# Issuing the weight loads of a decode layer in halves, from two DMA queues at the same time

## The chip, the cores and the metric

One core of one Trainium2 chip. The metric is the device time of the whole program on that core, in microseconds (us), lower is better. Some readings come from the trace's single records: the DMA packets (start, duration, bytes, queue) and the moments at which each of the 16 DMA engines reports its share of a load as landed. The trace doesn't number the engines, but on each engine a packet starts where the packet before it ended (to within about 20 ns), so one engine can be followed from packet to packet. These readings are given in plain tables; the profile's own lines stand in fences of their own.

## The reference, cut to what matters

One decode step for four sequences, in bfloat16: attention with a window of 2,048 cached keys, then a gated feed-forward layer. Nothing is used twice, so nearly all of the work is to read weights and cache once.

```python
def reference(A_x, A_k_cache, A_v_cache, A_wq, A_wo, B_x, B_w1, B_w3, B_w2):
    # x: 4 x 1 x 1024; k_cache, v_cache: 4 x 4 x 8192 x 128, the last 2048 keys count
    # wq: 1024 x 4096, wo: 4096 x 1024, w1, w3: 1024 x 3584, w2: 3584 x 1024
    h  = x + attention(layernorm(x), k_cache, v_cache, wq) @ wo
    n  = layernorm(h)
    return h + (silu(n @ w1) * (n @ w3)) @ w2
```

The core reads 55.6 MB for it: wq 8.4, K 8.4, V 8.4, wo 8.4, w1 7.3, w3 7.3, w2 7.3 MB.

## The kernel before

All big loads go through one ring buffer of 160 KiB per partition, in the order of a plan, all from the sync queue. A region is loaded again as soon as the matmuls that read it are done. Weights lie row after row inside a partition, so a load of m rows is one contiguous run per partition: 64 KiB for wo, 56 KiB for w1.

```python
    def load_rows(at, src, n, r0, m):
        t = ring[:, at : at + m * n]
        nc.sync.dma_start(out=t, in_=src[:, r0 * n : (r0 + m) * n])
        return [t[:, k * n : (k + 1) * n] for k in range(m)]
    # ... load_kv, load_side, load_tail: cut
    plan = [
        # ... wq in two loads, three small ones: cut
        ("k", load_kv, (64 * KIB, A_k_cache, 0)),
        ("k", load_kv, (96 * KIB, A_k_cache, 2)),
        ("v", load_kv, (128 * KIB, A_v_cache, 0)),
        ("v", load_kv, (0, A_v_cache, 2)),
        ("wo", load_rows, (32 * KIB, wo_v, D, 0, 32)),
        ("w1", load_rows, (96 * KIB, w1_v, N_F, 0, 8)),
        ("w3", load_rows, (0, w3_v, N_F, 0, 4)),
        ("w3", load_rows, (28 * KIB, w3_v, N_F, 4, 4)),
        ("w2", load_rows, (56 * KIB, w2_v, D, 0, 17)),
        ("w2", load_rows, (90 * KIB, w2_v, D, 17, 7)),
        ("w2", load_rows, (104 * KIB, w2_v, D, 24, 3)),
        ("w2", load_rows, (110 * KIB, w2_v, D, 27, 1)),
    ]
```

The end of the kernel (cut; comments added here):

```python
    gate_up("w1", g_ps)                               # 64 matmuls
    nc.scalar.activation(out=eg[:], in_=g_ps[:, :, :HF], func=ACT.Exp, scale=-1.0)
    nc.vector.tensor_scalar_add(out=eg[:], in0=eg[:], scalar1=1.0)
    nc.vector.reciprocal(out=eg[:], in_=eg[:])
    nc.vector.tensor_tensor(out=gs[:], in0=g_ps[:, :, :HF], in1=eg[:], op=ALU.mult)
    gate_up("w3", u_ps)                               # 64 matmuls
    nc.vector.tensor_tensor(out=hg[:], in0=u_ps[:, :, :HF], in1=gs[:], op=ALU.mult)
    nc.vector.transpose(out=hgT, in_=hg)              # then 112 matmuls with w2 into y2_ps
    nc.scalar.copy(out=res[:], in_=y2_ps[:])
    nc.scalar.dma_start(out=out_flat, in_=res)
```

Of the kernel before, what the change touches and what calls it, by code (L numbers as in the profile page):

```python
# [19 lines left out]
def kernel(  # L20
# [13 lines left out]
    nc = tc.nc  # L34

    B, _, D = A_x.shape
# [47 lines left out]
    wo_v = A_wo.rearrange("(p i) n -> p (i n)", i=IO)  # L84
    w1_v = B_w1.rearrange("(p i) n -> p (i n)", i=KC)
    w3_v = B_w3.rearrange("(p i) n -> p (i n)", i=KC)
    w2_v = B_w2.rearrange("(p i) n -> p (i n)", i=IF)
    ring = stream.tile([P, RING], BF16)

    def load_rows(at, src, n, r0, m):  # L90
# [2 lines left out]
        nc.sync.dma_start(out=t, in_=src[:, r0 * n : (r0 + m) * n])  # L93
        return [t[:, k * n : (k + 1) * n] for k in range(m)]

    def load_kv(at, src, b):

        out = []
        for k in range(BS):
            v = ring[:, at + k * JK * Dh : at + (k + 1) * JK * Dh]  # L100
            nc.sync.dma_start(
                out=v,
                in_=src[b + k, :, Sk - W : Sk, :].rearrange("g (pp j) d -> pp g (j d)", pp=PK),
            )
            out.append(v.rearrange("p (j d) -> p j d", d=Dh))
        return out

    N_Q, N_F = Hq * Dh, F
# [13 lines left out]
    def load_tail(at, src, n, r0, m):  # L122
# [4 lines left out]
    KIB = 512  # L127
# [4 lines left out]
        ("side", load_side, SETS[2]),  # L132
        ("wq", load_tail, (32 * KIB, wq_v, N_Q, 4, 4)),
        ("k", load_kv, (64 * KIB, A_k_cache, 0)),
        ("k", load_kv, (96 * KIB, A_k_cache, 2)),
        ("v", load_kv, (128 * KIB, A_v_cache, 0)),
        ("v", load_kv, (0, A_v_cache, 2)),
        ("wo", load_rows, (32 * KIB, wo_v, D, 0, 32)),
        ("w1", load_rows, (96 * KIB, w1_v, N_F, 0, 8)),
        ("w3", load_rows, (0, w3_v, N_F, 0, 4)),  # L140
        ("w3", load_rows, (28 * KIB, w3_v, N_F, 4, 4)),
        ("w2", load_rows, (56 * KIB, w2_v, D, 0, 17)),
        ("w2", load_rows, (90 * KIB, w2_v, D, 17, 7)),
        ("w2", load_rows, (104 * KIB, w2_v, D, 24, 3)),
        ("w2", load_rows, (110 * KIB, w2_v, D, 27, 1)),
    ]
# [3 lines left out]
    def load_next(n=1):  # L150
        for _ in range(n):
            if cursor[0] < len(plan):
                kind, f, args = plan[cursor[0]]
                loaded.setdefault(kind, []).extend(f(*args))
                cursor[0] += 1
# [19 lines left out]
    for c in range(2):  # L175
# [8 lines left out]
        out=xn[:], in0=x_sb[:], scalar1=mv[:, 0:1], scalar2=rstd[:, 0:1],  # L184
# [14 lines left out]
    for r0, ne, ns in SETS:  # L199
# [3 lines left out]
            out=xs[:, len(sl) : len(sl) + ns, : ne * 4].rearrange("b l (i s) -> b l i s", s=4),  # L203
            in_=v[:, KC - 1, :, :, :],
        )
        for l in range(ns):
            nc.tensor.transpose(
                out=ts_ps[: ne * 4, len(sl), :], in_=xs[:, len(sl), : ne * 4], identity=ident[:B, :B]
# [4 lines left out]
    for _, ne, ns in SETS:  # L213
# [14 lines left out]
        out=perm[:].rearrange("p (h dq) -> p h dq", dq=JG),  # L228
        in_=ident[:].rearrange("p (dq h) -> p h dq", dq=JG),
# [12 lines left out]
    for j in range(2, JG):  # L242
        nc.vector.tensor_tensor(
            out=same[:, 0, :], in0=same[:, 0, :], in1=ident[:, j * QD : (j + 1) * QD], op=ALU.add
# [6 lines left out]
    for kc in range(KC):  # L251
        wq_t = loaded["wq"][kc]
        for hf in range(CQ // 512):
            for g in range(JG):
                c0 = g * CQ + hf * 512
                n = min(512, N_Q - CE - c0) if kc == KC - 1 else 512
# [23 lines left out]
    for r in range(REP):  # L280
        nc.tensor.transpose(out=qt_ps[:, r, :], in_=q_sb[:, r * Dh : (r + 1) * Dh], identity=ident[:])
    nc.vector.tensor_copy(
        out=qz[:, :, : Hkv * QD].rearrange("p b (g z) -> p b g z", g=Hkv)[:, :, :, :REP],
        in_=qt_ps[:].rearrange("p r (g x) -> p x g r", g=Hkv)[:, :B, :, :],
# [10 lines left out]
    def emit_scores(u):  # L295
        b, n = units[u]
        kT_v = kT_tiles[u][:].rearrange("d j (pp g) -> d g j pp", g=Hkv)
        for g in range(Hkv):
            z0 = (b * Hkv + g) * QD
            nc.tensor.matmul(  # L300
                scores_ps[QD * g : QD * (g + 1), n * 512 : (n + 1) * 512],
                lhsT=qz_v[:, z0 : z0 + QD],
                rhs=kT_v[:, g, :, :],
                start=(b == 0),
                stop=(b == B - 1),
            )

    nt = 0
    for u, (b, n) in enumerate(units):
        k_v = loaded["k"][b]  # L310
        kT = ktpool.tile([P, NJ, P], BF16, tag="kT")
        for t in range(NJ // TB):
            kt_ps = psA.tile([P, TB, P], BF16, tag=f"kt{nt % 4}")
            for jj in range(TB):
                nc.tensor.transpose(  # L315
                    out=kt_ps[:, jj, :], in_=k_v[:, n * NJ + t * TB + jj, :], identity=ident[:]
                )
            if nt % 2 == 0:
                nc.vector.tensor_copy(out=kT[:, t * TB : (t + 1) * TB, :], in_=kt_ps[:])  # L319
            else:  # L320
                nc.scalar.copy(out=kT[:, t * TB : (t + 1) * TB, :], in_=kt_ps[:])  # L321
            nt += 1
        kT_tiles.append(kT)
        if u >= 1:
            emit_scores(u - 1)
        if u == NSB * BS - 1:
            load_next()
    emit_scores(len(units) - 1)


# [7 lines left out]
        out=Pm[:], in_=scores_ps[:], func=ACT.Exp, bias=nmax[:], scale=1.0, accum_out=rsum[:]  # L338
# [6 lines left out]
    for c in range(NSB):  # L345
# [4 lines left out]
        for g in range(Hkv):  # L350
            if g % 2 == 0:
                nc.vector.tensor_scalar(  # L352
                    out=z[:, :, g, :], in0=pt_ps[:], scalar1=mask[:, g : g + 1], scalar2=None, op0=ALU.mult
# [10 lines left out]
        out=Dm[:], in0=ident[:].rearrange("p (g b r) -> p b g r", g=Hkv, b=B),  # L364
# [38 lines left out]
    for i in range(IO):  # L403
# [34 lines left out]
        out=hn[:], in0=h1[:], scalar1=tot[:, 0:1], scalar2=rstd2[:, 0:1],  # L438
# [5 lines left out]
        out=hnT[:].rearrange("p k x -> p (k x)"), in_=hn[:].rearrange("q (c k) -> q k c", k=KC)  # L444
# [5 lines left out]
    def gate_up(kind, out_ps):  # L450
        for k in range(KC):
            for hf in range(2):
                for j in range(JG):
                    c0 = j * CF + hf * HF
                    nc.tensor.matmul(  # L455
                        out_ps[QD * j : QD * (j + 1), hf, :HF],
                        lhsT=hnT[:, k, :],
                        rhs=loaded[kind][k][:, c0 : c0 + HF],
                        start=(k == 0),
                        stop=(k == KC - 1),  # L460
                    )
            if kind == "w1" and k == RQ - 1:
                load_next(3)

    gate_up("w1", g_ps)
    eg = wide.tile([P, 2, HF], FP32, tag="w4k")
    nc.scalar.activation(out=eg[:], in_=g_ps[:, :, :HF], func=ACT.Exp, scale=-1.0)
    nc.vector.tensor_scalar_add(out=eg[:], in0=eg[:], scalar1=1.0)
    nc.vector.reciprocal(out=eg[:], in_=eg[:])  # L469
    gs = wide.tile([P, 2, HF], FP32, tag="w4k")  # L470
    nc.vector.tensor_tensor(out=gs[:], in0=g_ps[:, :, :HF], in1=eg[:], op=ALU.mult)
    gate_up("w3", u_ps)
    hg = act.tile([P, 2, HF], BF16)
    nc.vector.tensor_tensor(out=hg[:], in0=u_ps[:, :, :HF], in1=gs[:], op=ALU.mult)
# [3 lines left out]
        out=hgT[:].rearrange("p i x -> p (i x)"),  # L478
        in_=hg[:].rearrange("q s c -> q (s c)").rearrange("q (c i) -> q i c", i=IF),
# [47 lines left out]
```

## Time and profile before

| | before |
|---|---|
| time, median | 137.94 us (137.84 to 138.09, 4 runs) |
| span of the profiled run | 136.1 us |
| bytes moved, DMA packets | 55.75 MB, 2,789 |
| last byte of w2 landed | 132.77 us |

From the page of the kernel before: the DMA engines' busy share in tenths and the GB/s moved, in 40 slices of the span, then packets, and the queues (packets, MB, share of 16 engines' time). q1 is the sync queue, q10 ScalarE's.

```profile
DMA  5999999999999999999979999989899999989970
GB/s 156 463 464 404 404 438 405 424 428 438 433 428 419 429 443 428 429 522 477 462 327 443 481 409 404 477 371 477 354 430 426 438 455 442 430 389 419 421 288 5
DMA packets 2789, 55.75 MB, mean 410 GB/s; under 512 B 311, under 2 KB 471, under 8 KB 731
...
q1 hardware_dynamic: 2731, 55.58, 95.6%
...
q10 hardware_dynamic: 48, 0.02, 0.1%
```

The DMA engines are nearly full (8 to 9 tenths, one slice at 7) from the second slice to the last but two. That is the fact about this kernel. The same by stretches (stretch, length, busy time of PE, PEld, DVE, ACT, POOL with counts; then granted clock, DMA share, GB/s), kernel before:

```profile
60.00:100.00 40.00, 18.24 (x407) 13.43 (x411) 13.40 (x30) 10.45 (x14) 0.00 (x0) 0.62 1.01 434
100.00:125.00 25.00, 10.79 (x120) 4.80 (x113) 10.26 (x5) 2.20 (x2) 0.00 (x0) 0.64 1.00 431
```

431 to 434 GB/s with a DMA share of 1.0 (429 from 30 to 60 us). The Trainium skill ("DMA: Bandwidth & Descriptors", Specifications) gives 435 GB/s as the fabric's ceiling, and the trace agrees. (The same table's limit of about 358 GB/s per core at the HBM does not bind here, with one core in use.)

The waits of TensorE in the kernel before (who, for what: us in total, times, longest):

```profile
PE u_ps L455 <- DMA ring<-in_B_w_dram: 8.2, 2, 5.3
PE y_ps L485 <- DMA ring<-in_B_w_dram: 8.1, 3, 7.1
...
PE g_ps L455 <- DMA ring<-in_B_w_dram: 5.2, 1, 5.2
```

TensorE waits for w1 (g_ps), w3 (u_ps) and w2 (y_ps of L485). The same view has one stall of 4.0 us in the attention's matmuls (OT_ps) for nothing that the profile shows; an instruction fetch falls into it. Here is the end in order of time, kernel before (start, duration, what, and in brackets the idle time before it and what ended it; the gate's exponential and reciprocal and other short work are left out):

```profile
98.92 5.51 PE L455 MATMUL g_ps<-ring,hnT 128*32 128x448 bf16 x64 [5.17 <-DMA ring<-in_B_w_dram]
...
115.83 3.18 PE L455 MATMUL u_ps<-ring,hnT 128*32 128x448 bf16 x32 [5.27 <-DMA ring<-in_B_w_dram]
...
120.18 1.70 DVE L477 STREAM_TRANSPOSE hgT<-hg 128x896 bf16<-128x896 bf16 x1
...
126.09 3.82 PE L485 MATMUL y_ps<-ring,hgT 128*32 128x256 bf16 x68 [7.08 <-DMA ring<-in_B_w_dram]
```

hgT (the hidden layer, transposed for the last product) is ready at 121.9 us, and w2 comes only at 126.1: 4.2 us of slack in the compute chain. The chain of waits ends so (start, duration, what), kernel before:

```profile
101.46 31.31 DMA ring<-in_B_w_dram
132.77 0.04 issue
132.81 0.32 PE y_ps L485 x4
133.13 0.02 issue
133.15 0.37 ACT res L495
```

After the last landing come only four matmuls, a cast and the output's store.

### The profile page before, as it was taken

To read this page: it belongs to the slowest core of one execution; us is meant where nothing else is said; L and a number is where in the kernel's file an instruction comes from. 1 tells how busy PE (TensorE), PEld (TensorE's weight loads), DVE (VectorE), ACT (ScalarE), POOL (GpSimd) and SP (SyncE) were. 2 spreads that over 40 slices of the span, in tenths; PEclk is the share of its full clock that TensorE was granted. 3 is DMA by queue.
4 is the path that set the end of the run, shared out by engine and by line. 5 is a ranking of instruction groups with operands and counts; after the bars stand their busy time and mean duration, and the time that the engine had idled before them with its cause. 6 is when DMAs were issued, how large, how long until landed. Compare 5 with 4: busy or idle time off the path is not lost.

```text
span 136.1 us, 2343 instructions
## 1 busy us (share of the span) xinstructions
PE 73.8 (54%) x1050; PEld 45.0 (33%) x1050; DVE 43.4 (32%) x79; ACT 31.1 (23%) x36; POOL 1.7 (1%) x8
## 2 busy tenths in 40 slices
PE   0202980979898989810535906793096440900960
PEld 0200220267474747400024905571043210300840
DVE  6820000044243434471984001206100695080000
ACT  3000000016555555518385200000002300000001
POOL 5000000000000000000000000000000000000000
PEclk9999999999999999997555555579757777555577
DMA  5999999999999999999979999989899999989970
GB/s 156 463 464 404 404 438 405 424 428 438 433 428 419 429 443 428 429 522 477 462 327 443 481 409 404 477 371 477 354 430 426 438 455 442 430 389 419 421 288 5
DMA packets 2789, 55.75 MB, mean 410 GB/s; under 512 B 311, under 2 KB 471, under 8 KB 731
## 3 DMA queue, kind: packets, MB, share of 16 engines
q1 hardware_dynamic: 2731, 55.58, 95.6%
q8 instruction: 8, 0.13, 0.3%
q10 hardware_dynamic: 48, 0.02, 0.1%
q14 instruction: 2, 0.02, 0.0%
HBM read 55.59 MB, written 0.01 MB: 408 GB/s over the span
## 4 chain that ended last, share of the span: by engine, by line
DMA 54%; PE 24%; ACT 11%; DVE 5%; SPq 2%; issue 1%; ACTq 0%
DMA ring<-in_B_w_dram 40%; DMA ring<-in_A_wq_dram 15%; PE kt_ps L315 10%; ACT kT L321 5%; PE scores_ps L300 5%; ACT z L356 3%; PE q_ps L259 3%; SPq L119 2%; PE g_ps L455 2%; DVE rmax L332 2%; ACT Pm L337 2%; PE OT_ps L378 2%; DVE pT L346 1%; DVE z L352 1%; ACT L337 1%
## 5 line engine op out<-in xcount | busy, mean ns | idle before, releaser
L321 ACT COPY kT<-kt_ps 128x1024 bf16<-128x1024 bf16 x16 | 15.9, 1013 | 13.1 <-PE kt_ps L315 13.1
L315 PE MATMUL kt_ps<-ident,ring 128*128 128x128 bf16 x256 | 17.8, 230 | 0.0
L315 PEld LDWEIGHTS <-ring 128*128 128x128 bf16 x256 | 15.8, 104 | 4.9 <-issue 4.9
L319 DVE COPY kT<-kt_ps 128x1024 bf16<-128x1024 bf16 x16 | 11.1, 692 | 16.2 <-PE kt_ps L315 16.2
L259 PE MATMUL q_ps<-ring,xnT 128*4 128x512 bf16 x63 | 7.2, 626 | 10.5 <-DMA ring<-in_A_wq_dram 10.5
L378 PE MATMUL OT_ps<-z,ring 128*128 128x32 bf16 x256 | 7.5, 188 | 9.0 <-ACT z L356 5.0
L455 PEld LDWEIGHTS <-hnT 128*32 128x32 bf16 x128 | 5.3, 137 | 19.3 <-issue 16.6
L300 PE MATMUL scores_ps<-kT,qz 128*32 128x512 bf16 x64 | 9.9, 610 | 2.9 <-ACT kT L321 2.9
L455 PE MATMUL u_ps<-ring,hnT 128*32 128x448 bf16 x64 | 6.4, 576 | 8.2 <-DMA ring<-in_B_w_dram 8.2
L378 PEld LDWEIGHTS <-ring 128*128 128x128 bf16 x256 | 7.4, 105 | 9.8 <-issue 9.7
L485 PE MATMUL y_ps<-ring,hgT 128*32 128x256 bf16 x112 | 5.8, 375 | 8.3 <-DMA ring<-in_B_w_dram 8.1
L455 PE MATMUL g_ps<-ring,hnT 128*32 128x448 bf16 x64 | 5.5, 529 | 5.2 <-DMA ring<-in_B_w_dram 5.2
L485 PEld LDWEIGHTS <-hgT 128*32 128x32 bf16 x112 | 4.5, 130 | 10.2 <-issue 5.9
L259 PEld LDWEIGHTS <-xnT 128*4 128x4 bf16 x63 | 2.0, 115 | 14.8 <-issue 14.7
L277 DVE TENSOR_SCALAR q_sb<-q_ps 128x512 bf16<-128x512 f32 x1 | 0.7, 692 | 19.5 <-PE q_ps L259 19.5
L495 ACT CAST res<-y_ps 128x256 bf16<-128x256 f32 x1 | 0.4, 372 | 26.4 <-PE y_ps L485 26.4
L356 ACT ACTIVATE z<-pt_ps,mask 128x512 bf16<-128x512 f32 x8 | 5.3, 687 | 3.5 <-DVE z L352 3.5
L348 PE MATMUL pt_ps<-pT,perm 128*128 128x512 bf16 x4 | 2.4, 608 | 6.8 <-DVE pT L346 6.8
L278 ACT ACTIVATE q_sb<-q_ps 128x512 bf16<-128x512 f32 x1 | 0.6, 597 | 23.6 <-DVE q_sb L277 23.6
L405 PE MATMUL y_ps<-ring,o 128*32 128x256 bf16 x128 | 5.5, 352 | 0.8 <-DVE o L394 0.8
L352 DVE TENSOR_SCALAR z<-pt_ps,mask 128x512 bf16<-128x512 f32 x8 | 5.5, 738 | 1.2 <-ACT z L356 0.8
L469 DVE RECIPROCAL eg<-eg 128x896 f32<-128x896 f32 x1 | 5.8, 5754 | 0.0
(79 smaller groups left out, 50.2 us busy)
## 6 DMA issues: line engine op xcount, KB each, us to landing
ring<-in_A_k_cache_dram SPq DMA_DIRECT2D x4, 2048.0 KB, 25.4
ring<-in_A_v_cache_dram SPq DMA_DIRECT2D x4, 2048.0 KB, 39.0
ring<-in_B_w_dram SPq DMA_DIRECT2D x1, 7168.0 KB
ring<-in_B_w_dram SPq DMA_DIRECT2D x2, 3584.0 KB, 23.3
ring<-in_B_w_dram SPq DMA_DIRECT2D x1, 4352.0 KB
ring<-in_A_wq_dram SPq DMA_DIRECT2D x1, 4096.0 KB, 12.1
ring<-in_A_wq_dram SPq DMA_DIRECT2D x1, 3968.0 KB, 19.8
ring<-in_B_w_dram SPq DMA_DIRECT2D x1, 1792.0 KB
```

The costliest lines, as they stand in the source:

```text
L259: nc.tensor.matmul(q_ps[QD * g : QD * g + B, hf * 512 : hf * 512 + n], lhsT=xnT[:, kc, :], rhs=wq_t[:, c0 : c0 + n], start=(kc == 0), stop ...
L300: nc.tensor.matmul(scores_ps[QD * g : QD * (g + 1), n * 512 : (n + 1) * 512], lhsT=qz_v[:, z0 : z0 + QD], rhs=kT_v[:, g, :, :], start=(b = ...
L315: nc.tensor.transpose(out=kt_ps[:, jj, :], in_=k_v[:, n * NJ + t * TB + jj, :], identity=ident[:])
L319: nc.vector.tensor_copy(out=kT[:, t * TB : (t + 1) * TB, :], in_=kt_ps[:])
L321: nc.scalar.copy(out=kT[:, t * TB : (t + 1) * TB, :], in_=kt_ps[:])
L352: nc.vector.tensor_scalar(out=z[:, :, g, :], in0=pt_ps[:], scalar1=mask[:, g : g + 1], scalar2=None, op0=ALU.mult)
L356: nc.scalar.mul(out=z[:, :, g, :], in_=pt_ps[:], mul=mask[:, g : g + 1])
L378: nc.tensor.matmul(OT_ps[:, b, :], lhsT=loaded["v"][b][:, j, :], rhs=PTz[j // NJ][:, (j % NJ) * B + b, :, :], start=(j == 0), stop=(j == J ...
L405: nc.tensor.matmul(y_ps[QD * j : QD * (j + 1), :], lhsT=o4[:, i, :, :].rearrange("p b s -> p (b s)"), rhs=loaded["wo"][i][:, j * CG : (j + ...
L455: nc.tensor.matmul(out_ps[QD * j : QD * (j + 1), hf, :HF], lhsT=hnT[:, k, :], rhs=loaded[kind][k][:, c0 : c0 + HF], start=(k == 0), stop=( ...
L469: nc.vector.reciprocal(out=eg[:], in_=eg[:])
L485: nc.tensor.matmul(y2_ps[QD * j : QD * (j + 1), :], lhsT=hgT[:, i, :], rhs=loaded["w2"][i][:, j * CG : (j + 1) * CG], start=False, stop=(i ...
```

## The change

Intent: let two queues feed the DMA engines with the weights, each with half of every load. wo becomes two loads of 16 rows, so that each is free to start with its own region; the last two small loads of w2 stay as they were and are issued later in the program (comments added here).

```diff
+    def load_two(at, src, n, r0, m):
+        h = m - m // 2
+        t = ring[:, at : at + m * n]
+        nc.sync.dma_start(out=t[:, : h * n], in_=src[:, r0 * n : (r0 + h) * n])
+        nc.scalar.dma_start(out=t[:, h * n :], in_=src[:, (r0 + h) * n : (r0 + m) * n])
+        return [t[:, k * n : (k + 1) * n] for k in range(m)]
...
-        ("wo", load_rows, (32 * KIB, wo_v, D, 0, 32)),
-        ("w1", load_rows, (96 * KIB, w1_v, N_F, 0, 8)),
-        ("w3", load_rows, (0, w3_v, N_F, 0, 4)),
-        ("w3", load_rows, (28 * KIB, w3_v, N_F, 4, 4)),
-        ("w2", load_rows, (56 * KIB, w2_v, D, 0, 17)),
-        ("w2", load_rows, (90 * KIB, w2_v, D, 17, 7)),
+        ("wo", load_two, (32 * KIB, wo_v, D, 0, 16)),
+        ("wo", load_two, (64 * KIB, wo_v, D, 16, 16)),
+        ("w1", load_two, (96 * KIB, w1_v, N_F, 0, 8)),
+        ("w3", load_two, (0, w3_v, N_F, 0, 4)),
+        ("w3", load_two, (28 * KIB, w3_v, N_F, 4, 4)),
+        ("w2", load_two, (56 * KIB, w2_v, D, 0, 17)),
+        ("w2", load_two, (90 * KIB, w2_v, D, 17, 7)),
...
-            load_next()                 # wo
+            load_next(2)
...
-                load_next(3)            # the last three loads of w2, in the gate's matmuls
+                load_next()
...
     nc.vector.reciprocal(out=eg[:], in_=eg[:])
+    load_next(2)
```

## The prediction

> **What bounds the kernel now.** The DMA engines, nearly everywhere. The queue table gives the sync queue 95.6% of 16 engines' span; the slice view has the DMA row at 9 from the third microsecond to about 131. The trace's single packets run back to back: 57,344 bytes (w1) take 2.116 us, 65,536 (wo) 2.418 us, so 27.1 GB/s per engine, 434 for 16; from 4 to 125 us I count 430 to 433 GB/s. The Trainium skill ("DMA: Bandwidth & Descriptors", Specifications) names 435 GB/s as the fabric ceiling; the trace agrees. The chain of waits ends in w2's last landing (132.77 us), four matmuls, the cast at 133.15 and the output's store. TensorE is busy 54% and waited 5.2 us for w1, 8.2 for w3, 8.1 for w2 (table of waits). Not DMA-bound: 2 us at the start, 3 at the end.
>
> **What the change does.** No bytes go or come. The same page (Issuing engines are not separate DMA queues) says that all queues share the 16 engines and that only issue time is saved; an issue takes 0.33 us here and lies long before its data. So no gain is in sight. Costs:
> 1. Shorter packets. wo goes from 65,536 to 16,384 bytes (0.611 us each): 32 x 0.611 against 8 x 2.418 = +0.2 us. w1, w3, w2 in halves: +0.3 us together (28,672 bytes 1.062, 14,336 bytes 0.535 us). About +0.5 us, wholly on the DMA's time.
> 2. Order. One queue was first come, first served; two share. In the built program wo's rows 8-15 go out on ScalarE's queue when the q matmuls end (27 us instead of 42.5), beside K, and rows 24-31 at 43 us beside K and V. K b=1 lands near 37 us instead of 32.3 (TensorE may wait 1 us), V's last near 72 instead of 62.7; it is needed at 76. No great loss.
> 3. At 76 us ScalarE's queue issues its half of w1 while the sync queue still has 2.6 MB of wo, then its own half of w1, ahead. Shared by packets, wo's rows 16-23 land near 90 (all of wo: 82.1 before), w1's rows 0-3, needed first, near 103 (98.7 before), the last of w3 near 121 (115.6 before). The gate stage starts 4 us later. Before, there was slack: hgT ended at 121.9, and TensorE waited until 126.1 for w2. I expect hgT at 126 to 128 and w2's 112 matmuls (5.96 us) to end about 1 us after the last load, not 0.3.
>
> So the lost order mostly eats slack; the bytes still set the end. On the critical path: +0.5 us of packets, +0.5 us of backlog.
>
> **Prediction: 138.9 us**, 8 in 10 between 137.6 and 140.6. Faster by over 2%: 0.03; within 2%: 0.87; slower by over 2%: 0.10.
>
> **What would show it.** Queue table: q10 with about 14 MB, q1 with the rest, together 95 to 97%; middle slices still at 430 GB/s. Timeline: first gate matmul near 103 instead of 98.9; the wait before the first w2 matmul shorter than 7.1 us or gone; last landing 132.8 to 133.5.
>
> **What would make it wrong.** If two queues run the engines faster than 434 GB/s, it gains 1 to 2 us. If sharing is unfair, or a ring starves while the other is held by a semaphore, w1 or w3 may come so late that the chain of exponential, reciprocal (5.75 us) and hgT is bare at the end: 141 or more. TensorE's instruction fetches (16 KB, a queue of their own) wait behind packets; one seems to have cost TensorE 4.0 us at 78 us. Shorter packets may shorten that, off the critical path.

## The result, and the profile after

| | before | after |
|---|---|---|
| time, median | 137.94 us (137.84 to 138.09, 4 runs) | 138.72 us (138.59 to 138.82, 4 runs) |
| ratio | 1 | 1.0055 (95%: 1.0038 to 1.0073) |
| DMA packets | 2,789 | 3,941 |
| last byte of w2 landed | 132.77 us | 133.57 us |

The ratio here and below is the mean time of one kernel's fast runs over the mean of the other's in the same rounds, so it is not quite the ratio of the medians. The change costs about 0.8 us: less than the 2% that would count as slower, but clear of noise. Where those 0.8 us are is plain at once: the last landing is 0.80 us later, and what follows it is the same (the cast starts at 133.95 instead of 133.15).

The page of the changed kernel, same lines as before:

```profile
DMA  5999999999999999999999999999999999999960
GB/s 156 460 461 431 409 417 403 440 416 436 436 426 431 416 436 440 412 438 431 431 431 426 426 468 419 455 407 427 410 419 436 424 436 434 425 452 390 426 248 2
DMA packets 3941, 55.75 MB, mean 407 GB/s; under 512 B 439, under 2 KB 599, under 8 KB 987
...
q1 hardware_dynamic: 2875, 41.16, 70.7%
q10 hardware_dynamic: 1056, 14.44, 24.8%
```

A quarter of the bytes now goes through ScalarE's queue, and the two shares add up to 95.5%, about what the one queue had (95.6%). The stretches, changed kernel:

```profile
60.00:100.00 40.00, 17.92 (x395) 13.40 (x396) 14.00 (x30) 10.45 (x14) 0.00 (x0) 0.58 1.00 429
100.00:125.00 25.00, 9.67 (x128) 4.66 (x128) 10.26 (x5) 2.20 (x2) 0.00 (x0) 0.70 1.01 430
```

429 and 430 GB/s where it was 434 and 431 (428 from 30 to 60 us): the second queue added nothing. The Trainium skill says so (same page, "Issuing engines are not separate DMA queues": the queues share the 16 engines, and only issue time is saved), and this trace agrees. The waits of TensorE, changed kernel:

```profile
PE u_ps L464 <- DMA ring<-in_B_w_dram: 10.5, 2, 6.5
...
PE g_ps L464 <- DMA ring<-in_B_w_dram: 8.0, 1, 8.0
PE y_ps L495 <- DMA ring<-in_B_w_dram: 7.1, 2, 6.2
```

TensorE waits 2.8 us longer for w1, 2.3 us longer for w3, and 1.0 us less for w2. The end in order of time, changed kernel:

```profile
101.15 4.53 PE L464 MATMUL g_ps<-ring,hnT 128*32 128x448 bf16 x64 [7.96 <-DMA ring<-in_B_w_dram]
...
118.34 2.96 PE L464 MATMUL u_ps<-ring,hnT 128*32 128x448 bf16 x32 [6.52 <-DMA ring<-in_B_w_dram]
...
122.48 1.70 DVE L487 STREAM_TRANSPOSE hgT<-hg 128x896 bf16<-128x896 bf16 x1
...
127.52 4.57 PE L495 MATMUL y_ps<-ring,hgT 128*32 128x256 bf16 x96 [6.21 <-DMA ring<-in_B_w_dram]
```

The gate stage is 2.2 us later and hgT 2.3 us later (124.2), but the first matmul with w2 still waits for its data, to 127.5: 3.3 us of slack are left. The end of the chain of waits, changed kernel:

```profile
116.03 17.54 DMA ring<-in_B_w_dram
133.57 0.04 issue
133.61 0.32 PE y_ps L495 x4
133.93 0.02 issue
133.95 0.37 ACT res L505
```

So the question for the experiments is not the order of the loads, but why the same 55.75 MB take 0.8 us longer. Two theories stood against each other. P: each packet costs its engine something whatever its length, and there are 1,152 more of them, 72 per engine. Q: a second queue costs the engines something.

### The profile page after: what moved, and what is told of

Its sections match the earlier page's. It is cut to its first block, busy times and chain, and to the rows that moved or that the text cites. A ratio compares the mean times of both kernels' runs of the same rounds, so it can differ in the third digit from the quotient of the medians.

```text
span 136.9 us, 2361 instructions
## 1 busy us (share of the span) xinstructions
PE 72.5 (53%) x1050; PEld 44.4 (32%) x1050; DVE 43.1 (31%) x79; ACT 31.2 (23%) x36; POOL 1.7 (1%) x8
## 2 busy tenths in 40 slices
DMA packets 3941, 55.75 MB, mean 407 GB/s; under 512 B 439, under 2 KB 599, under 8 KB 987
## 4 chain that ended last, share of the span: by engine, by line
DMA 67%; PE 15%; ACT 7%; DVE 5%; issue 2%; SPq 1%; ACTq 0%
DMA ring<-in_B_w_dram 33%; DMA ring<-in_A_k_cache_dram 25%; DMA ring<-in_A_wq_dram 9%; PE OT_ps L387 5%; PE kt_ps L324 4%; ACT z L365 3%; PE scores_ps L309 3%; PE y_ps L414 2%; DVE rmax L341 2%; ACT Pm L346 2%; DVE pT L355 1%; DVE z L361 1%; ACT L346 1%; SPq L109 1%; ACT kT L330 1%
## 5 line engine op out<-in xcount | busy, mean ns | idle before, releaser
L324 PE MATMUL kt_ps<-ident,ring 128*128 128x128 bf16 x256 | 19.3, 232 | 2.4 <-DMA ring<-in_A_k_cache_dram 1.6
L464 PEld LDWEIGHTS <-hnT 128*32 128x32 bf16 x128 | 4.7, 121 | 22.9 <-issue 19.5
L464 PE MATMUL u_ps<-ring,hnT 128*32 128x448 bf16 x64 | 5.1, 484 | 10.5 <-DMA ring<-in_B_w_dram 10.5
L464 PE MATMUL g_ps<-ring,hnT 128*32 128x448 bf16 x64 | 4.5, 454 | 8.0 <-DMA ring<-in_B_w_dram 8.0
L414 PE MATMUL y_ps<-ring,o 128*32 128x256 bf16 x128 | 6.3, 387 | 0.8 <-DVE o L403 0.8
```

The costliest lines, as they stand in the source:

```text
L324: nc.tensor.transpose(out=kt_ps[:, jj, :], in_=k_v[:, n * NJ + t * TB + jj, :], identity=ident[:])
L414: nc.tensor.matmul(y_ps[QD * j : QD * (j + 1), :], lhsT=o4[:, i, :, :].rearrange("p b s -> p (b s)"), rhs=loaded["wo"][i][:, j * CG : (j + ...
L464: nc.tensor.matmul(out_ps[QD * j : QD * (j + 1), hf, :HF], lhsT=hnT[:, k, :], rhs=loaded[kind][k][:, c0 : c0 + HF], start=(k == 0), stop=( ...
```

## The experiments

All were correct. Median and ratio are against the kernel before in the same rounds (138.04 us for the first four, 137.89 us for the last four, which ran later on another chip).

| run | what | time | ratio (95%) |
|---|---|---|---|
| e1_one_queue | the halves, all on the sync queue | 138.37 | 1.0024 (1.0011 to 1.0037) |
| e2_two_queues_whole | two queues, whole loads | 140.88 | 1.0185 (1.0145 to 1.0224) |
| e3_wo_2k | one queue, wo in 2,048-byte packets | 139.25 | 1.0084 (1.0071 to 1.0097) |
| e4_slack | the changed kernel, 2.2 us more work before hgT | 138.63 | 1.0036 (1.0024 to 1.0048) |
| e5_after_again | the changed kernel | 138.68 | 1.0052 (1.0039 to 1.0064) |
| e6_one_queue_again | as e1 | 138.38 | 1.0032 (1.0019 to 1.0044) |
| e7_wo_two_queues | the halves, only wo on two queues | 138.74 | 1.0058 (1.0044 to 1.0072) |
| e8_w_two_queues | the halves, all but wo on two queues | 138.64 | 1.0053 (1.0041 to 1.0066) |

Read beside it the landings of the last load (w2's last row), from the trace. A load is complete when all 16 DMA engines have reported; the table gives the mean of the 16 moments, and the last:

| kernel | queues at work | mean of 16 | last | last minus mean |
|---|---|---|---|---|
| before | one | 132.25 | 132.77 | 0.52 |
| e1_one_queue | one | 132.62 | 133.10 | 0.48 |
| e6_one_queue_again | one | 132.57 | 133.05 | 0.48 |
| e3_wo_2k | one | 133.42 | 133.97 | 0.55 |
| after | two | 132.49 | 133.57 | 1.08 |
| e5_after_again | two | 132.55 | 133.54 | 0.99 |
| e4_slack | two | 132.52 | 133.54 | 1.02 |
| e2_two_queues_whole | two | 132.22 | 133.21 | 0.99 |
| e7_wo_two_queues | two, for wo | 132.59 | 133.45 | 0.86 |
| e8_w_two_queues | two, but for wo | 132.55 | 133.65 | 1.10 |

### e1_one_queue: short packets, one queue

```diff
-        nc.scalar.dma_start(out=t[:, h * n :], in_=src[:, (r0 + h) * n : (r0 + m) * n])
+        nc.sync.dma_start(out=t[:, h * n :], in_=src[:, (r0 + h) * n : (r0 + m) * n])
```

> The changed kernel, but the second half of each load goes to the sync queue too: all the short packets, one queue. Theory P (packets: each packet costs its engine about 8.5 ns whatever its length; the change adds 1152 packet records, 72 per engine, so 72 x 8.5 ns = 0.61 us): 0.5 to 0.8 us over the kernel before, the packet time per engine near 131.27 us as in the changed kernel (130.67 before), last landing 133.3 to 133.6 us. Rival Q (the second queue costs time, by switching or by spreading the 16 engines apart): within 0.2 us of the kernel before, last landing 132.8.

Measured: 138.37 us, 0.33 over the kernel before, last landing 133.10, the sum of packet durations 131.16 us per engine. It lies between the two theories: packets cost something, but about half of what P expects of them. (Sums of durations here are those of q1, q8 and q10.) One thing by the way: with halves in order on one queue, w1's first half landed at 90.5 and the gate's matmuls began at 95.3, 5.9 us before those of the changed kernel. The end did not move for it; it waits for bytes.

### e2_two_queues_whole: two queues, no shorter packets

```diff
+    def load_act(at, src, n, r0, m):        # load_rows, issued from ScalarE's queue
+        t = ring[:, at : at + m * n]
+        nc.scalar.dma_start(out=t, in_=src[:, r0 * n : (r0 + m) * n])
+        return [t[:, k * n : (k + 1) * n] for k in range(m)]
-        ("w1", load_rows, (96 * KIB, w1_v, N_F, 0, 8)),
+        ("w1", load_act, (96 * KIB, w1_v, N_F, 0, 8)),
-        ("w3", load_rows, (28 * KIB, w3_v, N_F, 4, 4)),
+        ("w3", load_act, (28 * KIB, w3_v, N_F, 4, 4)),
-        ("w2", load_rows, (90 * KIB, w2_v, D, 17, 7)),
+        ("w2", load_act, (90 * KIB, w2_v, D, 17, 7)),
     # and the last two loads of w2 are issued after the reciprocal, as in the changed kernel
```

> The kernel before with its whole, long loads, but w1, the second half of w3 and the 7-row part of w2 go out on ScalarE's queue: two queues at work together, no packet shortened. Theory P: within 0.2 us of the kernel before, packet time per engine 130.67 us, last landing 132.7 to 133.0. Rival Q: 0.5 us or more over it. Both expect 430 GB/s from 100 to 120 us, so no gain of bandwidth from a second queue. If a queue that wakes up waits for a number of packets of the other (it waited 3.4 us behind packets of 16,384 bytes, 0.611 us each, about 5.6 packets), w1's first packet on ScalarE's queue comes 9 to 14 us after its issue, behind packets of 65,536 bytes (2.418 us each); if it waits for a number of bytes, 3 to 4 us. Either way w1 lands at 101 to 106 instead of 98.7, in slack.

Measured: 140.88 us (139.81 to 141.67), 2.8 over the kernel before. Q's "0.5 us or more" covers the number, but not for Q's reason; the profile shows where it comes from, and it isn't the bandwidth. The end in order of time, e2_two_queues_whole:

```profile
123.98 3.18 PE L461 MATMUL u_ps<-ring,hnT 128*32 128x448 bf16 x32 [12.27 <-DMA ring<-in_B_w_dram]
...
128.33 1.70 DVE L484 STREAM_TRANSPOSE hgT<-hg 128x896 bf16<-128x896 bf16 x1
...
130.09 5.94 PE L492 MATMUL y_ps<-ring,hgT 128*32 128x256 bf16 x112 [2.93 <-DVE hgT L484]
```

The first w2 matmul waits for hgT here, no longer for w2. The second half of w3 landed at 123.9 us instead of 115.8, because it stood on ScalarE's queue behind w1 while the sync queue was already moving w2, which is needed later. The slack was used up, and 112 matmuls (5.94 us) stood bare after hgT. This is the failure that the prediction names under "What would make it wrong" (w1 or w3 so late that the chain is bare at the end), in another kernel than the one predicted. In the changed kernel both queues carry the loads in the order of need, each its half, so the order stays nearly right (w1 complete at 101.1 us against 98.9 before, w3 at 118.3 against 115.8); with whole loads dealt out in turn it does not. My expectation "in slack" was wrong, although w1 landed at 105.7, within its range.

For P against Q its landings count: the mean of the 16 engines is that of the kernel before (132.22 against 132.25), as P expects without shorter packets; but the last engine is 0.99 us after the mean instead of 0.52. (A part of this is older than the second queue in this run: at 62.8 us, with V, one engine was already 0.38 us behind the next, 0.19 in the kernel before.) The stretch from 100 to 125 us moved 432 GB/s, so no gain of bandwidth there either.

How long a waking queue waits for its first packet: w1 was issued at 74.37, and its first packets started between 78.8 and 80.3 on the 16 engines, 4.4 to 6.0 us later, behind packets of 65,536 bytes. In the changed kernel it was 3.4 us on the first engine and 4.7 on the last, behind packets of 16,384 bytes. So it is not a fixed number of packets (9 to 14 us had been expected then); it is nearer to a fixed number of bytes (3 to 4 us), but above it.

### e3_wo_2k: the packet's cost by itself, 249 more of them

```diff
+    def load_short(at, src, n, r0, m):
+        t = ring[:, at : at + m * n]
+        for odd in range(2):
+            nc.sync.dma_start(
+                out=t.rearrange("p (k two n) -> p two k n", two=2, n=n)[:, odd],
+                in_=src[:, r0 * n : (r0 + m) * n].rearrange("p (k two n) -> p two k n", two=2, n=n)[:, odd],
+            )
+        return [t[:, k * n : (k + 1) * n] for k in range(m)]
-        ("wo", load_rows, (32 * KIB, wo_v, D, 0, 32)),
+        ("wo", load_short, (32 * KIB, wo_v, D, 0, 32)),
```

> The kernel before, one queue, but wo in two loads of every other row, so that its packets are 2,048 bytes (0.084 us each) instead of 65,536 (2.418 us): 256 per engine instead of 8. Theory P: 256 x 0.084 - 8 x 2.418 = +2.16 us on each engine, so 2.0 to 2.4 us over the kernel before, with all of it in the landing of wo (82.1 to about 84.2) and kept to the end. Rival: if packet lengths do not matter, as in theory Q, 0.

From its page, to set beside the 2,789 packets of the kernel before:

```profile
DMA packets 6773, 55.75 MB, mean 406 GB/s; under 512 B 327, under 2 KB 487, under 8 KB 4843
```

Measured: 139.25 us, 1.21 over the kernel before; the mean landing rose by 1.17 us, the last by 1.20. So packet length matters, and Q alone is out; but the cost is a little over half of what the packets' durations say. The sum of durations did rise as expected, by 2.09 us per engine (130.67 to 132.76). The stretches of this run show why both are true:

```profile
60.00:100.00 40.00, 16.82 (x399) 12.90 (x403) 13.61 (x30) 10.45 (x14) 0.00 (x0) 0.59 1.03 422
```

16 engines can't be busy for more than the whole time. The view counts a packet where it starts, so the edges alone can make 1.01, as in the kernel before; but with packets cut at the edges, the share from 63 to 80 us, where wo moves, is 1.05 here (1.00 in the kernel before), at 408 GB/s. So the recorded durations of packets that follow each other overlap. A duration contains some time in which the engine is already at the next packet, so a sum of durations overstates what short packets cost. From this run a packet costs 1.17 us / 249 = 4.7 ns. (The run also reads every other row at a time; a cost of that order of reading would be within the figure.) Times the change's 72 it is 0.34 us, and the one-queue twin with just these packets measured 0.33 us (e1) and its mean landing 0.37 and 0.32 us later (e1, e6). The Trainium skill ("DMA: Bandwidth & Descriptors", "Why small descriptors are slow") has a fixed overhead of about 3 cycles per packet inside an engine; at the 850 MHz that the page gives for the fabric that would be 3.5 ns (an estimate from that page, which doesn't say that this part runs at the fabric's clock). This trace has 4.7 ns, of the same order.

### e4_slack: is the compute chain exposed?

```diff
-    nc.vector.tensor_tensor(out=hg[:], in0=u_ps[:, :, :HF], in1=gs[:], op=ALU.mult)
+    for _ in range(3):
+        nc.vector.tensor_tensor(out=hg[:], in0=u_ps[:, :, :HF], in1=gs[:], op=ALU.mult)
```

> The changed kernel with the product before hgT computed three times instead of once on VectorE (two more of 1.09 us): hgT ends at about 126.4 instead of 124.2 us. If the wait for w2 before the first w2 matmul (6.2 us, to 127.5) is real slack, the time stays within 0.2 us of the changed kernel, 0.6 to 0.9 over the kernel before. If the compute chain was exposed, as the third point of the prediction had it, it is up to 2.2 us longer.

The end in order of time, e4_slack:

```profile
121.47 3.34 DVE L485 TENSOR_TENSOR hg<-u_ps,gs 128x896 bf16<-128x896 f32 x3 [5.71 <-PE u_ps L464]
124.84 1.70 DVE L488 STREAM_TRANSPOSE hgT<-hg 128x896 bf16<-128x896 bf16 x1
...
127.49 4.71 PE L496 MATMUL y_ps<-ring,hgT 128*32 128x256 bf16 x96 [6.08 <-DMA ring<-in_B_w_dram]
```

Measured: 138.63 us, 0.59 over the kernel before (a hair under the 0.6 to 0.9 expected), so no slower than the changed kernel itself. hgT ended at 126.5 instead of 124.2 us, and the first w2 matmul started where it had, at 127.49, released by the DMA. The slack is real, and no part of the 0.8 us is in the compute chain.

### e5 to e8: the second queue's share

At this point two parts were on the table: the mean of the engines is later by the packets (0.3 us), and in each kernel with two queues the last engine is late by about another half microsecond. In the changed kernel this straggler was still within 0.2 us of its neighbour at 77 us and 0.57 us behind at 101 us, so I took it to come from w1's two queues. The last four runs set the changed kernel and its one-queue twin side by side, and tested that.

```diff
 # e7_wo_two_queues, in load_two
-        nc.scalar.dma_start(out=t[:, h * n :], in_=src[:, (r0 + h) * n : (r0 + m) * n])
+        q = nc.scalar if n == D and m == 16 else nc.sync            # only wo
+        q.dma_start(out=t[:, h * n :], in_=src[:, (r0 + h) * n : (r0 + m) * n])
 # e8_w_two_queues
+        q = nc.scalar if not (n == D and m == 16) else nc.sync      # all but wo
```

> The changed kernel as it is, in the same rounds as its one-queue twin. Theory P+Q, formed from the first four runs: the short packets move the mean of the 16 engines' last landings (132.25 before, 132.5 to 132.6 with short packets), and two queues at work hold one engine back, so that the last landing is 1.0 us after the mean instead of 0.5. Then 0.5 to 0.8 us over the kernel before, last landing near 133.55, 1.0 us after the mean. If the straggler was a chance of single profiles: last minus mean near 0.5 here and the same time as the one-queue twin.

Measured: 138.68 us, 0.79 over the kernel before, last landing 133.54, 0.99 after the mean: the straggler is no chance of one profile.

> The one-queue twin of the changed kernel again. Theory P+Q: 0.3 us over the kernel before, 0.2 to 0.4 us faster than the changed kernel in the same rounds, last landing near 133.1, 0.5 us after the mean of the 16 engines. Packets alone: the same time as the changed kernel.

Measured: 138.38 us, 0.30 us less than the changed kernel in the same rounds, last landing 133.05, 0.48 after the mean: as expected. Against the kernel before it is 0.49 us, more than the 0.3 expected, though its last landing is only 0.28 later. The rest is TensorE's: in the profiles of e1 and e6 the chain ends not with the last landing and 4 matmuls (0.32 us), but with the landing before it and 14 matmuls (1.07 us), at a granted clock of 0.50 from 132 to 134 us where the kernel before and the changed kernel had 1.00. So the cast starts 0.51 to 0.52 us after the last landing instead of 0.38. The twin's time therefore overstates what the packets cost, and the 0.30 us understates how much earlier its data came: 0.49 us (133.54 against 133.05).

> The converse: wo in its pieces on the sync queue, the second halves of w1, w3 and w2 on ScalarE's queue. Theory P+Q expects the changed kernel's time, 0.5 to 0.8 us over the kernel before, last landing near 133.55, 1.0 us after the mean. If wo's part was the cause: the one-queue twin's time.

Measured: 138.64 us, last landing 133.65, 1.10 after the mean. As expected, but see the next.

> All pieces as in the changed kernel, but only wo's second halves on ScalarE's queue (27 to 58 us); w1, w3 and w2 on the sync queue alone. In the changed kernel the last engine is still within 0.2 us of the next at 77 us and 0.57 us behind at 101 us, so the straggler comes with w1's two queues: theory P+Q expects the time of the one-queue twin, last landing near 133.1, 0.5 us after the mean. If any use of a second queue costs, or if wo's early start beside K does: the changed kernel's time.

Measured: 138.74 us, the changed kernel's time, last landing 133.45, 0.86 after the mean. The theory about w1 falls: wo on two queues is enough. What is more, the straggler was not there while two queues worked (27 to 58 us). The trace has the last four of the 16 landings of each load; around the place where it appears:

| kernel | load | last four landings |
|---|---|---|
| e7_wo_two_queues | w3, first quarter | 103.07, 103.08, 103.10, 103.17 |
| e7_wo_two_queues | w3, second quarter | 107.33, 107.35, 107.43, 107.95 |
| e6_one_queue_again | w3, first quarter | 103.09, 103.15, 103.16, 103.17 |
| e6_one_queue_again | w3, second quarter | 107.36, 107.39, 107.40, 107.41 |

One engine loses half a microsecond at once and never makes up for it. The trace has two kinds of packets that are not data and could take it: those of the kind "instruction", of 16,384 bytes on q8 (eight in a run) and of 8,192 bytes on q14 (two in the span). The first kind is not it. One starts at 102.66 us in e7, but e6 has the same at 102.87, and in both it falls on an engine that is ahead: of the 16 landings, those more than 0.8 us before the middle fall from six to five. The second kind fits (times in us; the count is that of ScalarE's instructions in the trace, DMA issues and waits included, begun before the second packet):

| kernel | queues | first packet of q14 | second | ScalarE's count | last landing of w2 |
|---|---|---|---|---|---|
| before | one | 60.18 | 135.57 | 64 | 132.77 |
| e1_one_queue | one | 60.16 | 135.84 | 64 | 133.10 |
| e6_one_queue_again | one | 60.11 | 135.79 | 64 | 133.05 |
| e3_wo_2k | one | 59.99 | 136.81 | 64 | 133.97 |
| after | two | 60.76 | 87.96 | 65 | 133.57 |
| e5_after_again | two | 61.88 | 89.95 | 65 | 133.54 |
| e4_slack | two | 60.72 | 87.93 | 65 | 133.54 |
| e2_two_queues_whole | two | 58.51 | 93.86 | 62 | 133.21 |
| e8_w_two_queues | two | 60.22 | 93.29 | 66 | 133.65 |
| e7_wo_two_queues | two, for wo | 61.24 | 104.23 | 63 | 133.45 |

The time of the second packet differs by up to 49 us, ScalarE's count only from 62 to 66 (at the first packet it is 38 to 41); SyncE's goes from 24 to 55 and VectorE's from 82 to 101, and GpSimd had long finished. So the packet seems to go with ScalarE's own instruction stream, and each load issued from ScalarE to bring it forward: in all six kernels with two queues it falls where the DMA engines are full, in all four with one queue after the last landing. Its cost can be read too: on the engine that carries it, it takes 0.31 us, and the next packet takes 0.25 to 0.49 us longer than others of its size, 0.55 to 0.80 us in all. Followed from packet to packet, that engine ends its share of w1's first half last in the changed kernel (100.17 us, the next 99.67), in e4 (100.14, 99.71) and in e8 (100.79, 100.28), and in e7 it is last from w3's second quarter on (w2's first load, second half: 126.36, the next 125.94). In e5 it is last but one there (98.02, 98.52), and in e2 I could not follow it.

So the straggler is not shown to be a cost of sharing between queues; ten profiles point to an instruction fetch that ScalarE's extra instructions bring forward. That is read from traces, not tested: no run gave ScalarE more instructions without a second queue, such as the one-queue twin with a dozen more of them. Why the packet falls on an engine that has no time in hand stays open. What is shown is the amount: 0.3 us in time between the changed kernel and its one-queue twin, 0.49 us in the last landing (e5 against e6), and 0.3 to 0.6 us in how far the last engine is behind the mean.

### A version that beats both?

The experiments point the other way only by a little: fewer, longer packets. The two loads of w3 in one would save 8 packets per engine, 8 x 4.7 ns = 0.04 us (an estimate from e3's figure), which no run here could tell from noise. None was run.

## Why the prediction was right or wrong

The time was predicted as 138.9 us, within 137.6 to 140.6; it is 138.72. The frame held: the kernel is bound by its bytes at the engines' ceiling, two queues add no bandwidth, and the change costs a fraction of a per cent. The sum of 0.5 + 0.5 us was near the measured 0.8 us by luck: of its two terms one was mis-sized and the other was not there; a third thing took its place.

- "About +0.5 us, wholly on the DMA's time" for shorter packets: the mechanism is right, the size was too large. Measured: 0.32 to 0.37 us in the mean landing, 0.28 to 0.33 in the last (e1, e6), 4.7 ns per packet (e3); in time 0.33 us (e1) and 0.49 (e6), of which 0.13 to 0.14 us in the profiles is TensorE's slower end. The failure is in the costing: durations of single packets were subtracted, and these overlap. (It also left out the eight further loads' completion packets, 8 of the 72 per engine.)
- "+0.5 us of backlog" at the end, with hgT at 126 to 128 and the wait for w2 nearly gone: wrong. hgT ended at 124.2, the wait was 6.2 us, and 2.2 us of added work changed nothing (e4). The step that failed is the landing times under two queues: wo's rows 16-23 at 85.2 us and not 90, w1's rows 0-3 at 101.1 and not 103, the last of w3 at 118.3 and not 121. ScalarE's half of w1, issued at 76.58, moved its first packet only at 79.98; the estimate had it share at once. The sharing itself was as assumed: the queues took turns, one packet each. One engine, followed from 79.98 to 83.31 us, began packets of 28,672 bytes (ScalarE's), 16,384 (sync), 28,672, 16,384 and 28,672; over all engines the bytes from 80 to 84 us went 39 to the sync queue, 61 to ScalarE's. (The Trainium skill, "DMA: Bandwidth & Descriptors", "Queues, rings and completion order", has the engines take turns between queues by packets; the trace agrees.)
- Not foreseen: the last DMA engine about half a microsecond further behind the others in each kernel that used two queues, which is 0.3 us of time (e5 against e6). A load is complete with its slowest engine, and the prediction counted 16 equal ones. What makes it late is most likely an instruction fetch of ScalarE, brought forward by its extra instructions; that is argued from the traces, not tested.
- Point 2 was right: K's second batch landed at 35.7 us (predicted 37), TensorE waited 1.6 us for K (predicted 1), V's last batch landed at 72.3 (predicted 72), and none of it reached the end.
- The instruction fetch: TensorE's stall of 4.0 us at 78 us in the attention's matmuls shrank to 2.1 us, to 2.2 us in the one-queue twin (e1) and to 2.0 us with wo in 2,048-byte packets (e3); with two queues and long packets it was 3.3 us (e2). So most of it goes with the shorter packets, not with the second queue. It lies in slack.

## What to carry to other kernels

When the DMA engines are full and at their ceiling, a load cut in two and issued from two queues is the same bytes in more packets: look at the share and the GB/s of the queues first, and if the share is at 95% and the rate is flat, leave the issue side alone. If two queues are used for other reasons, let both carry every load, in order of need; whole loads dealt to the queues in turn let later data overtake earlier data (e2, 2.8 us). Ask also what the issuing engine's extra instructions bring with them, and where that falls: look at the packets of the kind "instruction" in the trace. And cost a packet by a run with many more of them, not by differences of recorded durations.

## What the Trainium skill lacked or had wrong

- "DMA: Bandwidth & Descriptors", Issuing engines are not separate DMA queues: it says rightly that a second queue saves only issue time, but not that it can cost. Here it cost 0.3 us of 138 (e5 against e6), in a last engine that ended 0.9 to 1.1 us after the mean of the 16 instead of 0.5. With it an 8,192-byte instruction packet of q14 came at 88 to 104 us, in the full stretch, instead of after 135; it takes 0.55 to 0.80 us of one DMA engine.
- The same page, Queues, rings and completion order: no page has what a queue waits that wakes while another is busy. Here its first packet started 3.4 to 4.7 us after the issue behind packets of 16,384 bytes, and 4.4 to 6.0 us behind packets of 65,536 bytes.
- The same page, Why small descriptors are slow: the fixed cost per packet is told as cycles, and packing together as worth it only at 256 bytes and less. In a kernel bound by the engines, 4.7 ns per packet (e3) counted with packets of 2,048 bytes (1.2 us) and could be measured even with 14,336 to 28,672 bytes (0.3 us for 72 packets per engine).
- No page says that recorded packet durations overlap: 2.09 us more of them per engine were 1.17 us of time (e3).
